# Two attention blocks on one core: another order of TensorE's work in the first block, and a shorter cycle at one place in the second

## The chip, the core and the metric

The kernel runs on one core of a Trainium2 chip. The metric is the device time of one execution in microseconds. Before the change it is 1818.95 us, the median of three runs (1818.33 to 1819.58).

## What is computed

Two independent multi-head attention blocks, A and B, each on an input of 2048 tokens by 512, with 32 heads of 16; their outputs stand beside each other in the result. A looks back over a window of 256 tokens, B looks at all tokens.

```python
qkv = (x @ wqkv).reshape(B, S, 3, H, Dh)             # S=2048, D=512, H=32, Dh=16
scores = einsum("bhqd,bhkd->bhqk", q, k) * Dh**-0.5
# A alone: mask = (i - j >= 0) & (i - j < 256), scores = where(mask, scores, -1e9)
p = softmax(scores, axis=-1)
o = einsum("bhqk,bhkd->bhqd", p, v)                  # then joined over heads
out = o @ wo                                         # result: concat([a, b], -1)
```

## The kernel before

**The work.** The heads are taken in groups of four, the queries in chunks of 512. A unit is (block, group, chunk): 8 groups by 4 chunks make 32 units in A and 32 in B. The work on TensorE comes in four kinds.

- Projections and output products (`products`, L217): matmuls over 128 rows and 512 columns, twelve in a row for one 128x512 tile (four slices, three products each, because every operand is split into a high and a low part). One projection is one letter `p` of the order of block A or, in block B, a tile fed in pieces by the letter `x`.
- Maxima: scores of queries against keys, once over, for the row maximum that softmax subtracts. In A this is `max_item` (L454), read by VectorE (L459, or L463 and L464). In B it is `max2` (L406), read by VectorE's maximum reduction at L410. A large `M` handles two heads at once in two banks of PSUM that are kept for it; a small `m` handles one head in a bank that it shares in turn. The maxima of a unit become rows of its query operand by a small transpose (L492 in A, L539 in B; the letters `t` and `T`).
- Scores (`scores`, L572): the scores again, transposed, with the maxima subtracted by the extra rows. ScalarE takes the exponential of each 128x512 bank (L579); in A GpSimd cuts the edge of the window out of it (L589). These are the letters `s`.
- Weighing (`weigh` L618 in A, `weigh2` L603 in B): the exponentials times the values, four heads in four column groups. These are the letter `w` and, in B, digits that give how many 128-query pieces are weighed.

Scores and maxima use 48 to 51 rows of the array, so two of them run side by side; below, both kinds are called narrow matmuls. Weighing uses 32 columns for each head.

**What sets the order.** The schedule is manual. Every engine gets its instructions in the order in which the Python code issues them, and waits on semaphores alone. Block A follows two written tables: `ORDER_A` (L65) is a string of the letters above, and `ORDER_P` (L50) names the projections, those of B's queries, keys and values among them, in the order in which the `p`s take them. The loop at L964 reads them, and a model of the engines' clocks inside the kernel (class `Model`) decides when loads and the second halves of projections are issued between the letters.

Block B runs in cycles. The loop at L1099 picks one of five strings for each turn: `ORDER`, the plain cycle of two key steps; `ORDER_F`, eight key steps with room for a tile (letters `x`: output products of A); `ORDER_B`, which is the plain cycle without its last `M`; and `LAST` and `LAST_F`, once there are no maxima left. A key step is four scores and four weighing pieces.

```python
ORDER   = "ssm4mssMs2msms2TsM"
ORDER_B = "ssm4mssMs2msms2Ts"
ORDER_F = "msMs2mssm2ssMms4ssMms4 ..."
```

`due()` (L1096) tells whether an output product is to be fed now. A cycle with a tile may only begin when the key step is a multiple of eight. In the kernel before, the key steps go: eleven plain cycles from step 2, sixteen cycles with a tile from step 24, then 170 plain ones, two `LAST` and five `LAST_F`. The rule for `ORDER_B` asked for `due()` at step 22, where it did not hold yet, so that string never stood anywhere.

Of the kernel before, what the change touches and what calls it, by code (L numbers as in the profile page):

```python
# [20 lines left out]
HG = 4  # L21
# [15 lines left out]
STEP = 2.36  # L37
# [3 lines left out]
ORDER = "ssm4mssMs2msms2TsM"  # L41
ORDER_B = "ssm4mssMs2msms2Ts"
ORDER_F = "msMs2mssm2ssMms4ssMms4ssMms4ssMsm4ssMms4mssMsxxxxxxTxxMsmss4MssmsxxxxsMsms4s"
# [4 lines left out]


ORDER_P = (  # L50
# [4 lines left out]
    "Bk31 Bq30 Bq33 Bq32 Bq20 Bk23 Bk30 Bq31 Bk11 Bk33 Bk32 Bq12 ").split()  # L55
FIRST = 4.0
FINAL = 34.5
LOADS = 4.0
# [4 lines left out]


ORDER_A = (  # L65
    "pppppppmpmmpmmpmmmptpmmpmmpsmspmmpmsppmmpmmmpmmtpmsswmmmpsmswtmmpmswssmpmmtpmswmsmpmsswsmwssmpmswmss"
    "wtmmpsmmpsmwmmmpmsmwsmwsstpsmswmmmpsmswwssmpsmsptwsmmpmsmwwmsmpsmsptsmwmsmwsmsmsmwssmmwtssmwmmmpmswm"
    "msptsmmswmmmpmmswsmsmwsmtwsspssmwmmmpmsswtmswmsmpmsswmmswsmmptssmwmmspmsmwmswmsmpsmswmmmptmsmmmpmsmw"
    "smmswmswstmmpmsmsmwsmwsmssmwtmmmpmsmsmwssmwsmtswsmmpmswsmswmmtpsmswmmmpmsswmmmpmmtpsmswwmssptmswsmmw"
    "sspmswmmmpmsswsmtpmmswsmwsmmpmsssmwsmswmmtpssmwmmmpsmswmmmpsmswwsmmptsmwmsmpmsmwmsptsmwmsmpsmsptmswm"  # L70
    "mmpssmwmsmwsmsmwmsmptsmwmsmpsmswmmmpssmwmmmpssmtwwssmpmsswsmwsmmptsewmmmpsempsmswsemwsmptsewmmmpemsp"
    "mmswsmtwssepssmwmmmpempesswemmpssmwwsesptsmwemmpesmwmmpssmwsseptmsmpmmmpesmwsmwsmmpemmpmmmpemmpssmws"
    "mmptsmwmmmpSmSwmSmwSm")
LAND = 700
LATE = 1000
LAND_V = 2000
# [72 lines left out]
def attention_kernel(ctx: ExitStack, tc: tile.TileContext, xT, wqk, wv, wo, out):  # L149
# [9 lines left out]
    M = Model()  # L159
    ready = {}  # L160
    obank = [None]
    ns = 0
# [232 lines left out]
    def max2(g, c, qt, kc, heads, ps):  # L395

        m = maxima(1, g, c).rearrange("p (a r) q k -> p a r q k", a=2)
        early = g == 0 and c == 0 and heads[0] < 2
        if not early:
            follow(("k", 1, g))  # L400
            follow(("q", 1, g, c))
        for n, j in enumerate(heads):
            r, a = divmod(j, 2)
            rows = slice(ROW[a], ROW[a] + KS)
            q, k = (qe[0], ke()) if early else (opq[1, g, c][:, r], opk2(g)[:, r])
            nc.tensor.matmul(ps[:, n], q[rows, 128 * qt:128 * qt + 128], k[rows, kc * QC:kc * QC + QC], start=True,  # L406
                             stop=True)
            t = M.pe("h", 118, 0 if early else loaded(1, g, c))
        r, a = divmod(heads[0], 2)
        nc.vector.tensor_reduce(out=m[:, a:a + len(heads), r, qt, kc], in_=ps, axis=AX.X, op=ALU.max)  # L410
        return M.run("DVE", 65 + 533 * len(heads), t)
# [318 lines left out]
    proj = []  # L730
# [23 lines left out]
    def settle():  # L754

        while soon and soon[0][0] <= M.t["PE"]:
            heapq.heappop(soon)[2]()
# [14 lines left out]
    def room(hold=False):  # L772

        if slot[0]:
            if slot[2] is not None:
                return None, view(("s", slot[2] ^ 1))
            slot[1] ^= 1
            if hold:
                slot[2] = slot[1]
            return None, view(("s", slot[1]))  # L780
        while bank() >= M.NEVER:
            advance()
        b = M.take("e")
        return b, view(b)
# [7 lines left out]
    def pop():  # L792
        now[0], _, f, a = heapq.heappop(todo)
        f(*a)
        made.add((f, *a))

    gen = [None, None]
# [19 lines left out]
    def operands(it):  # L817

        f, b, *a = it
        if f == project_qk:  # L820
            keys = [(("w", b, a[0], a[1]), ("x", b, a[2], i)) for i in range(4)]
            t = slots_st[0] - 2700 + LAND_V
        elif f == project_v:
            keys = [(("w", b, "v", i), ("x", b, a[0], i)) for i in range(4)]
            t = slots_v[0] - 2700 + LAND_V
        else:
            keys = [(("w", b, "o", i), ("o", b, i, a[0])) for i in range(4 if len(a[1]) == 1 else 3)]
            t = 0
        at = [max(ready.get(x, M.NEVER) for x in k) for k in keys]
        return M.NEVER if max(at) >= M.NEVER else max(t, *(x - FEED * i * (f != project_out) for i, x in enumerate(at)))  # L830
# [115 lines left out]
    nm = k = nb = ne = n1 = 0  # L946
# [141 lines left out]
    mx = [(NA + 1 + i // 16, *units[NA + 1 + i // 16][1:], *divmod(i % 16, NQC)) for i in range(16 * turn)]  # L1088
    ns, nq, nm, fed = n1, n1 - 8, AHEADM, 0
    half, odd, full = 2 * AHEADM, None, set()  # L1090
    t0 = M.t["PE"] - 1000 * ns // HG * STEP
    rows, order = [], ORDER
    for u, g, c, qt, kc in mx[:AHEADM]:
        chunk_max(g, c, qt, kc)

    def due():  # L1096
        return gen[0] or proj and proj[0][0] <= ns // HG * STEP and operands(proj[0][3]) <= M.t["PE"]

    while nq < 4 * len(steps):  # L1099
        if nm == len(mx) and len(M.banks["e"]) == 3:  # L1100
            M.banks["e"] += [M.t["PE"] + 4000] * 2
        if nm == len(mx):
            order = LAST_F if due() and not rows else LAST
        else:
            f, g = order == ORDER_F, ns // HG % 8
            order = ORDER_F if due() and g == 0 and nm + 8 <= len(mx) else ORDER
            if order == ORDER and not f and g == 6 and due() and nm + 10 <= len(mx):
                order = ORDER_B
        for x in order:
            k = ns // HG  # L1110
            if x == "s" and k < len(steps):
                if ns % HG == 0:
                    t = k * STEP
                    M.t["PE"] = max(M.t["PE"], t0 + int(1000 * k * STEP))
                    settle()
                    while todo and todo[0][0] <= t:
                        pop()
                scores(1, *steps[k], ns % HG)
                ns += 1
            elif x in "Mm" and (half < 2 * len(mx) or x == "m" and odd is not None):  # L1120
                if x == "M":
                    y = half
                    half += 1
                    max2(*mx[y // 2][1:], (2 * (y % 2), 2 * (y % 2) + 1), ps_all[:, 3:5])
                elif odd is None:
                    y, odd = half, half
                    half += 1
                    max2(*mx[y // 2][1:], (2 * (y % 2),), room()[1][:, None])
                else:
                    y, odd = odd, None  # L1130
                    max2(*mx[y // 2][1:], (2 * (y % 2) + 1,), room()[1][:, None])
                if y != odd:
                    full.add(y)
                while {2 * nm, 2 * nm + 1} <= full:
                    u, g, c, qt, kc = mx[nm]
                    chunk_max(g, c, qt, kc)
                    nm += 1
                    if nm % 16 == 0:
                        low_finish(g, c)
                        rows.append((k + 1, (1, g, c)))  # L1140
            elif x == "T":
                if rows and rows[0][0] + (nm == len(mx)) <= k:
                    max_rows(*rows.pop(0)[1])
            elif x == "x" and (gen[0] or due()):
                now[0] = k * STEP
                advance()
                fed += 1
                if fed == 12:
                    fed = 0
                    advance()  # L1150
                    if nm < len(mx):
                        t0 += 2410
            elif x.isdigit():
                if 0 <= nq < 4 * len(steps):
                    g, c, kt = steps[nq // 4]
                    q = nq % 4
                    weigh2(g, c, kt, 128 * q, 128 * (q + int(x)))
                    if kt == NT - 1 and q + int(x) == 4:
                        unit_end(1, g, c)
                nq += int(x)  # L1160
# [29 lines left out]
```

## Time and profile before

| | |
|---|---|
| runs | 1818.33, 1818.95, 1819.58 us |
| profiled execution, its own time | 1819.65 us |
| its span, first to last instruction | 1817.9 us |
| mean granted TensorE clock | 0.998 |
| TensorE matmul busy | 1798.2 us (99%) |
| VectorE / ScalarE / GpSimd busy | 1515.2 / 1420.0 / 688.8 us |
| block A with the projections | from 10.2 us to about 541 us |
| block B, first plain cycles | about 541 to 592 us |
| block B, cycles with a tile, then plain ones, then the last | from 592 us on |

A busy engine here is one with an instruction under way; matmuls overlap and their ends are modelled, so a stall of TensorE shows in the distance between the starts of its groups better than in the busy time. In the rows of the timeline the first number is the start in us, the second how long the group lasted, and `x8` the number of instructions; a bracket gives the idle time ahead and what ended it.

### The profile page before, as it was taken

How to read it: one execution, taken by the hardware profiler on the slowest of the kernel's cores; microseconds unless marked ns; L12 is line 12 of the kernel's file. 1: busy time of each engine (PE TensorE's matmuls, PEld its weight loads, DVE VectorE, ACT ScalarE, POOL GpSimd, SP SyncE). 2: the span in 40 equal slices, each digit the busy share in tenths (PEclk: the TensorE clock that was granted, in tenths of full speed). 3: DMA queues.
4: the chain of work that ended last, by engine and by line, in shares of the span. 5: the costliest groups of instructions: out<-in, count | busy, mean ns of one | idle time of the engine just before them, and what ended most of it. 6: DMA issues, size and time to landing. Idle time of an engine off the chain costs nothing. (4 is left out here: it accounts for less than half of the span.)

```text
span 1817.9 us, 38163 instructions
## 1 busy us (share of the span) xinstructions
PE 1798.2 (99%) x13992; PEld 901.4 (50%) x13992; DVE 1515.2 (83%) x2189; ACT 1420.0 (78%) x2773; POOL 688.8 (38%) x2054
## 2 busy tenths in 40 slices
PE   7999999999999999999999999999999999999999
PEld 5766666666664444444444444444444444444446
DVE  4655676766689889999989999999999999999911
ACT  4367777565659788888889988998898998899883
POOL 0167787554655453223222423332222333222310
PEclk9999999999999999999999999999999999999999
DMA  7756767454553225111300311030030121000012
GB/s 239 198 177 200 225 206 220 152 164 140 180 182 104 71 74 117 45 42 40 75 28 26 74 47 39 29 78 17 16 76 29 35 63 37 17 24 15 30 34 97
DMA packets 128569, 166.47 MB, mean 92 GB/s; under 512 B 22946, under 2 KB 58258, under 8 KB 128370
## 3 DMA queue, kind: packets, MB, share of 16 engines
q1 hardware_dynamic: 128382, 164.04, 31.2%
q8 instruction: 110, 1.80, 0.4%
q14 instruction: 77, 0.63, 0.1%
HBM read 94.49 MB, written 68.19 MB: 89 GB/s over the span
## 5 line engine op out<-in xcount | busy, mean ns | idle before, releaser
L579 ACT ACTIVATE p<-ps_all 128x512 f32<-128x512 f32 x2432 | 1257.8, 598 | 163.1 <-PE ps_all L572 116.0
L410 DVE TENSOR_REDUCE mt<-ps_all 128x1 f32<-128x512 f32 (+1 forms) x1482 | 1203.4, 884 | 53.3 <-PE ps_all L406 38.2
L572 PE MATMUL ps_all<-oq,opk 51*128 51x512 f32 (+3 forms) x2752 | 739.4, 406 | 2.4 <-ACT p L579 2.1
L406 PE MATMUL ps_all<-opk,oq 48*128 48x512 f32 x2016 | 636.3, 433 | 1.0 <-DVE mt L410 1.0
L603 PE MATMUL ps_all<-p,vt 128*32 128x256 f32 (+1 forms) x5672 | 586.8, 487 | 0.0
L572 PEld LDWEIGHTS ps_all<-oq,opk 51*128 51x128 f32 (+1 forms) x2752 | 376.8, 185 | 227.7 <-ACT p L579 196.0
L406 PEld LDWEIGHTS ps_all<-opk,oq 48*128 48x128 f32 x2016 | 303.1, 185 | 277.7 <-issue 149.7
L517 POOL TENSOR_TENSOR md<-mt,mm 128x4 f32<-128x4 f32 x372 | 75.9, 204 | 612.2 <-DVE mt L410 611.2
L589 POOL TENSOR_SCALAR_AFFINE_SELECT p<-p 128x256 f32<-128x256 f32 x480 | 178.9, 406 | 221.9 <-ACT p L579 220.4
L603 PEld LDWEIGHTS ps_all<-p,vt 128*32 128x32 f32 x5672 | 112.7, 108 | 218.1 <-issue 208.1
L217 PE MATMUL ps_all<-x,w 128*128 128x512 f32 x768 | 195.1, 404 | 10.3 <-ACT w L170 10.2
L463 DVE COPY_PREDICATED ps_all<-mone,ps_all 128x256 f32<-128x256 uint16 x224 | 95.0, 424 | 85.8 <-PE ps_all L454 84.1
L217 PEld LDWEIGHTS ps_all<-x,w 128*128 128x128 f32 x768 | 141.2, 190 | 50.5 <-ACT w L170 10.2
L464 DVE TENSOR_REDUCE mt<-ps_all 128x2 f32<-128x512 f32 x224 | 155.2, 693 | 7.7
L279 ACT ACTIVATE raw<-ps_all 128x512 f32<-128x512 f32 x56 | 33.5, 598 | 108.8 <-PE ps_all L217 105.9
L217 PE MATMUL ps_all<-w_o,x_o 128*128 128x512 f32 x384 | 102.3, 407 | 0.2 <-ACT ob L715 0.2
L217 PE MATMUL ps_all<-w_v,x 128*128 128x512 f32 x384 | 96.4, 400 | 0.3 <-DVE w_v L171 0.3
L618 PE MATMUL ps_all<-p,vt 128*32 128x384 f32 (+2 forms) x1408 | 96.4, 390 | 0.0
L518 POOL TENSOR_SCALAR md<-md 128x4 f32<-128x4 f32 x372 | 81.7, 220 | 32.6
L454 PE MATMUL ps_all<-opk,oq 48*128 48x384 f32 (+2 forms) x512 | 88.1, 373 | 1.3 <-DVE mt L464 1.1
L519 POOL TENSOR_TENSOR mm<-mm,md 128x4 f32<-128x4 f32 x372 | 74.8, 201 | 31.0
L217 PEld LDWEIGHTS ps_all<-w_o,x_o 128*128 128x128 f32 x384 | 68.0, 188 | 26.9 <-issue 8.0
(63 smaller groups left out, 718.3 us busy)
## 6 DMA issues: line engine op xcount, KB each, us to landing
parts<-st SPq DMA_DIRECT2D x64, 512.0 KB
opk<-parts SPq DMA_DIRECT2D x128, 128.0 KB
oq<-parts SPq DMA_DIRECT2D x128, 128.0 KB
od<-ou SPq DMA_DIRECT2D x64, 256.0 KB
vd<-vst SPq DMA_DIRECT2D x32, 272.0 KB
opk<-parts SPq DMA_DIRECT2D x128, 64.0 KB
oq<-parts SPq DMA_DIRECT2D x128, 64.0 KB
t<-od SPq DMA_DIRECT2D x32, 256.0 KB
```

Of the source, the lines that this page charges most:

```text
L217: nc.tensor.matmul(ps, l(u), r(v), start=start and k == 0, stop=stop and k == n - 1)
L406: nc.tensor.matmul(ps[:, n], q[rows, 128 * qt:128 * qt + 128], k[rows, kc * QC:kc * QC + QC], start=True, stop=True)
L410: nc.vector.tensor_reduce(out=m[:, a:a + len(heads), r, qt, kc], in_=ps, axis=AX.X, op=ALU.max)
L454: nc.tensor.matmul(two[:, a, 0:w], opq[b, g, c][rows, r, 128 * qt:128 * qt + 128], opk2(g)[rows, r, t0:t1], start=True, stop=True)
L463: nc.vector.copy_predicated(two[:, :, 256:384], later, two[:, :, 0:128])
L464: nc.vector.tensor_reduce(out=m[:, :, r, qt, 0], in_=two[:, :, 128:384], axis=AX.X, op=ALU.max)
L518: nc.gpsimd.tensor_scalar(d, d, 0.0, None, op0=ALU.max)
L572: nc.tensor.matmul(ps[x][:, col:col + n1], opk2(g)[rows, pr, 128 * k:128 * k + 128], opq[b, g, c][rows, pr, q0:q0 + n1], start=True, stop= ...
L579: nc.scalar.activation(p[:, a0 + x, :w], ps[x][:, :w], AF.Exp, scale=SCALE)
L589: nc.gpsimd.affine_select(out=v, in_=v, pattern=[[0, 2], [sign, 128]], compare_op=ALU.is_ge, fill=zero_fill, base=base, channel_multiplier ...
L603: nc.tensor.matmul(o[32 * j:32 * j + 32, q0:q1], vt[(g // 2) % 2][:, kt, vc:vc + 32], pts[1, g, c, kt, j // 2][:, j % 2, q0:q1], start=kt ...
L618: nc.tensor.matmul(o[32 * j:32 * j + 32, q0:q0 + w], vt[(g // 2) % 2][:, kt, vc:vc + 32], pts[b, g, c, m, j // 2][:, j % 2, col:col + w], ...
```

## The change

Two things change. The tables `ORDER_A` and `ORDER_P` hold another order for block A: the same letters and the same projections, placed differently. And in block B the rule that picks `ORDER_B` looks two key steps ahead and applies once, to the first place that fits.

```diff
 ORDER_P = (
-    "Ak00 Aq00 Av00 Av11 Aq01 Av20 Ak01 Aq02 Av02 Av33 Av13 Ak02 Av03 Av01 Ak03 Av31 Aq03 Av22 Av23 Av21 Av10 "
+    "Ak00 Aq00 Av13 Av03 Aq01 Av12 Aq02 Ak01 Av00 Av22 Av01 Ak02 Av02 Av21 Aq03 Ak03 Av10 Av11 Av32 Av20 Av23 "
...
 ORDER_A = (
-    "pppppppmpmmpmmpmmmptpmmpmmpsmspmmpmsppmmpmmmpmmtpmsswmmmpsmswtmmpmswssmpmmtpmswmsmpmsswsmwssmpmswmss"
+    "pppppppmmpmpmmpmmmptppmmmpsmspmmpmmpmmpmsmtpssmwmsmpsmswwmmmptmswsmmpmsmpmswmmspmsspmmptsmwmmmptsmws"
...
-    rows, order = [], ORDER
+    rows, shorter = [], True
...
-    def due():
-        return gen[0] or proj and proj[0][0] <= ns // HG * STEP and operands(proj[0][3]) <= M.t["PE"]
+    def due(ahead=0):
+        d = (ahead + ahead / 20) * STEP
+        return gen[0] or proj and proj[0][0] <= ns // HG * STEP + d and operands(proj[0][3]) <= M.t["PE"] + 1000 * d
...
-            f, g = order == ORDER_F, ns // HG % 8
+            g = ns // HG % 8
             order = ORDER_F if due() and g == 0 and nm + 8 <= len(mx) else ORDER
-            if order == ORDER and not f and g == 6 and due() and nm + 10 <= len(mx):
-                order = ORDER_B
+            if shorter and g == 6 and due(2):
+                order, shorter = ORDER_B, False
```

In the changed kernel the key steps go: ten plain cycles, one `ORDER_B` at step 22, sixteen cycles with a tile from step 24, 171 plain ones, one `LAST` and five `LAST_F`. The maximum left out at step 22 is made up at the end: every later maximum comes half a letter pair later, and the last ones fall into the plain cycle at step 492.

**TensorE where the first cycle with a tile begins** (step 24 of block B; `oq_0_1` is the query operand of the unit whose scores are made, L572, `oq_0_2` that of the unit whose maxima are made, L406, `p` the exponentials that are weighed, L603). Before:

```order
L603 MATMUL ps_all<-p_0_1_5_0_7005,vt_76 32x256 x2
L603 MATMUL ps_all<-p_0_1_5_1_7018,vt_76 32x256 x2
L572 MATMUL ps_all<-oq_0_1_5847,opk_74 128x512
L406 MATMUL ps_all<-opk_74,oq_0_2_6059 128x512 x3
L572 MATMUL ps_all<-oq_0_1_5847,opk_74 128x512
L406 MATMUL ps_all<-opk_74,oq_0_2_6059 128x512 x2
L572 MATMUL ps_all<-oq_0_1_5847,opk_74 128x512
L603 MATMUL ps_all<-p_0_1_6_0_7034,vt_76 32x256 x2
```

The same place in the changed kernel, between the same two weighing groups:

```order
L603 MATMUL ps_all<-p_0_1_5_0_7005,vt_76 32x256 x2
L603 MATMUL ps_all<-p_0_1_5_1_7018,vt_76 32x256 x2
L572 MATMUL ps_all<-oq_0_1_5834,opk_74 128x512
L406 MATMUL ps_all<-opk_74,oq_0_2_6097 128x512
L572 MATMUL ps_all<-oq_0_1_5834,opk_74 128x512
L406 MATMUL ps_all<-opk_74,oq_0_2_6097 128x512 x2
L572 MATMUL ps_all<-oq_0_1_5834,opk_74 128x512
L603 MATMUL ps_all<-p_0_1_6_0_7034,vt_76 32x256 x2
```

Of the three L406 matmuls after the first score, two are gone: they were the `M` that ended the plain cycle. What stays is the small `m` and the `M` of the cycle with a tile.

**TensorE in block A, scores of group 1, chunk 2** (`oq_1_2`; `oq_2_0` and `oq_2_1` belong to maxima, L454). Before:

```order
L618 MATMUL ps_all<-p_1_2_0_1_1692,vt_76 32x384 x2
L572 MATMUL ps_all<-oq_1_2_1091,opk_75 128x384 x2
L572 MATMUL ps_all<-oq_1_2_1091,opk_75 128x128 x2
L454 MATMUL ps_all<-opk_74,oq_2_0_1455 128x384 x2
L572 MATMUL ps_all<-oq_1_3_1298,opk_75 128x128 x2
L572 MATMUL ps_all<-oq_1_3_1298,opk_75 128x384 x2
L454 MATMUL ps_all<-opk_74,oq_2_0_1455 128x384 x2
L572 MATMUL ps_all<-oq_1_3_1298,opk_75 128x128 x2
L572 MATMUL ps_all<-oq_1_3_1298,opk_75 128x384 x2
L454 MATMUL ps_all<-opk_74,oq_2_1_1622 128x384 x2
L618 MATMUL ps_all<-p_1_2_1_0_1706,vt_76 32x256 x2
```

In the changed kernel, the scores of the same unit:

```order
L454 MATMUL ps_all<-opk_74,oq_2_0_1531 128x384 x4
L572 MATMUL ps_all<-oq_1_2_1115,opk_75 128x256 x4
L217 MATMUL ps_all<-x_0_0_115,w_2_0_953 128x512 x3
L217 MATMUL ps_all<-x_0_1_118,w_2_0_953 128x512 x3
L217 MATMUL ps_all<-x_0_2_123,w_2_0_953 128x512 x3
L217 MATMUL ps_all<-x_0_3_126,w_2_0_953 128x512 x3
L572 MATMUL ps_all<-oq_1_2_1115,opk_75 128x384 x2
L572 MATMUL ps_all<-oq_1_2_1115,opk_75 128x128 x2
L454 MATMUL ps_all<-opk_74,oq_2_0_1531 128x384 x2
L572 MATMUL ps_all<-oq_1_2_1115,opk_75 128x384 x2
L572 MATMUL ps_all<-oq_1_2_1115,opk_75 128x128 x2
L618 MATMUL ps_all<-p_1_2_0_0_1655,vt_76 32x128 x2
```

Before, eighteen narrow matmuls stood in one piece here, with no projection near; now a projection stands between the score steps, and the longest piece of this unit has ten.

More of the change, by code (lines that the diff above doesn't have):

```diff
@@ L50 @@
 ORDER_P = (
[4 rows of a table removed]
-    "Bk31 Bq30 Bq33 Bq32 Bq20 Bk23 Bk30 Bq31 Bk11 Bk33 Bk32 Bq12 ").split()
[4 rows of a table added]
+    "Bq11 Bq20 Bk31 Bq31 Bq13 Bq33 Bk32 Bk33 Bk30 Bk21 Bq32 Bq30 ").split()
 FIRST = 4.0
@@ L65 @@
 ORDER_A = (
-    "pppppppmpmmpmmpmmmptpmmpmmpsmspmmpmsppmmpmmmpmmtpmsswmmmpsmswtmmpmswssmpmmtpmswmsmpmsswsmwssmpmswmss"
[L67 to L73, printed above, removed]
+    "pppppppmmpmpmmpmmmptppmmmpsmspmmpmmpmmmpsmtpssmwmsmpsmswwmmmptmswsmmpmsmpmswmmspmsspmmptsmwmmmptsmws"
+    "mmpsmswsmwmsmptmswmsmwsspsmswmmmpsmswmswmmmptwssmpmsspmmswmmpsmswtmswmmspsmswmmsptsmwmsmwsmsmwssmwmm"
+    "spmmtpsmswmmmptmsswmmswswssspmmswmmwmspssmwmsmpmsswtmmmpmmspsmmwswmmmptsmsmwmsmptsmswmmmpsmmswmmswst"
+    "smswsmswmspmsmmwmswtssmwsmmpsmsmwmmswsmmswmmmptssmwmsmptsmsmwsmswmmmpmsswsmmpmswmmsptmswsmmpmmswmmpm"
+    "sswmswmsmptsmwmmmpssmpmmtpmmswsmwsmmpsmswsmswmmtpsmswmmmpsmswtsmswmswmsspsmwmsswsmwmsmptsmswmmmpsmsw"
+    "ssmwtmmmpsmmpmswmmmpmsstwsmswmmmpmsswmmmpmmtpsmmptmswmswsempmswsmmpmmswwesmpessptmswsmmpmsmwmswsemps"
+    "sewemsptssmwemmpseswmmmpesswsmswwsempmmtpemspseswsmwmmmpsempmmmpemmptssmwmmmpseswsewmmmpmmmpsmstwmsm"
+    "psmswmmmpmmSwSwmmSpSm")
 LAND = 700
```

6 rows, old and new, of the table ORDER_P are left out of this document.

## The prediction

> **What bounds the kernel now.** I read the page first, then the windows by stage, then TensorE's timeline wherever the distance between two starts was longer than elsewhere.
>
> ```profile
> span 1817.9 us, 38163 instructions
> PE 1798.2 (99%) x13992; PEld 901.4 (50%) x13992; DVE 1515.2 (83%) x2189; ACT 1420.0 (78%) x2773; POOL 688.8 (38%) x2054
> ```
>
> TensorE is the bound: 99% of the span. The same matmuls run before and after the change, so time can only come from stalls of TensorE, from its clock, and from the small price of going from one kind of matmul to another. The windows say where the stalls are.
>
> ```profile
> 100.00:160.00 60.00, 60.00 (x496) 39.70 (x495) 33.91 (x71) 39.59 (x78) 39.67 (x79) 1.00 0.63 193
> 160.00:280.00 120.00, 117.86 (x987) 75.59 (x988) 86.44 (x207) 88.19 (x175) 93.72 (x177) 1.00 0.68 206
> 280.00:540.00 260.00, 259.78 (x1998) 172.27 (x1996) 179.89 (x337) 156.87 (x309) 147.47 (x295) 1.00 0.56 172
> 592.00:604.00 12.00, 11.00 (x64) 4.09 (x62) 8.90 (x11) 6.48 (x13) 8.19 (x16) 0.72 0.26 67
> 1100.00:1300.00 200.00, 200.00 (x1721) 84.19 (x1714) 200.00 (x261) 180.20 (x355) 61.60 (x246) 1.00 0.14 37
> ```
>
> The columns are the window, its length, then busy time of PE, PEld, DVE, ACT and POOL, and near the end the granted clock. Two places stand out: 160 to 280 us in block A, and the twelve microseconds from 592, where the mean clock was 0.72. The plain cycles (1100 to 1300) have no idle TensorE, and a VectorE that is busy throughout: there the two are level.
>
> **The seam at 592 us.** Here the plain cycles end and the first cycle with a tile begins. TensorE's timeline:
>
> ```profile
> 590.22 0.64 PE L603 MATMUL ps_all<-p,vt 128*32 128x256 f32 x8
> 590.79 0.50 PE L406 MATMUL ps_all<-opk,oq 48*128 48x512 f32 x1
> 591.46 0.64 PE L603 MATMUL ps_all<-p,vt 128*32 128x256 f32 x8
> 592.03 0.50 PE L572 MATMUL ps_all<-oq,opk 51*128 51x512 f32 x1
> 592.03 0.94 PE L406 MATMUL ps_all<-opk,oq 48*128 48x512 f32 x3
> 592.81 0.40 PE L572 MATMUL ps_all<-oq,opk 51*128 51x512 f32 x1
> 594.21 0.50 PE L406 MATMUL ps_all<-opk,oq 48*128 48x512 f32 x2 [1.00 <-DVE mt L410]
> 594.55 0.40 PE L572 MATMUL ps_all<-oq,opk 51*128 51x512 f32 x1
> 594.88 0.64 PE L603 MATMUL ps_all<-p,vt 128*32 128x256 f32 x8
> 598.82 1.93 PE L603 MATMUL ps_all<-p,vt 128*32 128x512 f32 x8
> 600.69 0.79 PE L572 MATMUL ps_all<-oq,opk 51*128 51x512 f32 x2
> 603.46 0.50 PE L572 MATMUL ps_all<-oq,opk 51*128 51x512 f32 x2
> 604.36 1.07 PE L603 MATMUL ps_all<-p,vt 128*32 128x512 f32 x8
> 605.36 0.50 PE L572 MATMUL ps_all<-oq,opk 51*128 51x512 f32 x2
> ```
>
> At 594.21 the large `M` of the new cycle waits for VectorE: the plain cycle's last `M` (the L406 at 592.03) still holds the two banks. VectorE had no gap since 584.76, and a large reduction takes 1.22 us:
>
> ```profile
> 584.76 12.51 DVE L410 TENSOR_REDUCE mt<-ps_all 128x1 f32<-128x512 f32 x16
> 598.51 1.82 DVE L410 TENSOR_REDUCE mt<-ps_all 128x2 f32<-128x1024 f32 x2 [1.24 <-PE ps_all L406]
> ...
> L410 DVE TENSOR_REDUCE mt<-ps_all 128x2 f32<-128x1024 f32 x566 | 687.6, 1217 | 51.7 <-PE ps_all L406 38.0 <-PE ps_all L572 7.9
> ```
>
> What came after is odd: the same weighing of eight 512-column matmuls took 1.87 us (598.82 to 600.69) and 1.00 us later (604.36 to 605.36). Windows cut at the change of clock:
>
> ```profile
> 592.49:595.90 3.41, 2.41 (x20) 1.04 (x17) 3.41 (x4) 1.79 (x3) 3.19 (x4) 1.00 0.56 143
> 595.90:599.31 3.41, 3.41 (x22) 1.22 (x22) 2.16 (x4) 2.32 (x5) 3.09 (x7) 0.50 0.20 70
> 599.31:602.73 3.42, 3.42 (x18) 1.03 (x14) 1.80 (x3) 1.56 (x4) 1.51 (x5) 0.50 0.00 0
> 602.73:606.14 3.41, 3.41 (x28) 1.18 (x20) 2.87 (x5) 2.19 (x5) 0.00 (x0) 1.00 0.00 0
> ```
>
> The granted clock fell to 0.50 for 6.83 us, right after 3.41 us in which TensorE was busy for 2.41 (71%). So the stall costs twice: itself, and the slow clock behind it. It is the only slow stretch once the work runs: 6.83 us at half clock make 0.998 of the span's mean, which is what the run lists:
>
> ```profile
> core 0: 1817.9 us, clock 0.998
> ```
>
> **The change, term by term.**
>
> *The stall at the seam, -1.7 us.* Prices of undisturbed visits: narrow matmuls, four of them, 0.67 us (590.79 to 591.46); six of them, 0.90 (603.46 to 604.36). That is 0.20 for a visit and 0.235 for each pair side by side. The eight from 592.03 should have taken 0.20 + 4 x 0.235 = 1.14 and took 2.85 (to 594.88): 1.71 too long. With `ORDER_B` ahead, the `M` that held the banks is gone. The `M` before that is older, VectorE has 1.22 us less ahead of it, and the wait falls away; what is late next is the same VectorE, by at most what is left of its queue: 0 to 0.5 us, and I take 0. The pair of matmuls (0.235 us) is not saved, only made up at the end.
>
> *The slow clock, -3.0 us.* From 594.88 to 604.36 stand two 256-column weighings, two of 512 columns, four narrow matmuls once and six three times. At full clock: 2 x 0.57 (590.22 to 590.79) + 2 x 1.00 + 0.67 + 3 x 0.90 = 6.51 us. They took 9.48: 2.97 lost. If the clock stays up, all of it comes back, as VectorE even idled there (1.24 us at 598.51). From above the term is bounded by half of 6.83, 3.4 us; from below by nothing, if the clock falls all the same. I take 3.0, since the drop sits exactly behind the one window with so much idle TensorE.
> [...]
>
> *Block A's stalls, -1.5 us.* They come where many narrow matmuls stand in one piece, because ScalarE and VectorE cannot empty the banks as fast. In the order there are eight pieces of 12 to 18, all between 170 and 392 us. The first and the last:
>
> ```profile
> 168.95 0.44 PE L454 MATMUL ps_all<-opk,oq 48*128 48x384 f32 x2
> 169.83 1.07 PE L618 MATMUL ps_all<-p,vt 128*32 128x128 f32 x16
> 170.83 0.50 PE L572 MATMUL ps_all<-oq,opk 50*128 50x384 f32 x4
> 173.48 1.07 PE L618 MATMUL ps_all<-p,vt 128*32 128x256 f32 x16
> ...
> 389.71 0.50 PE L572 MATMUL ps_all<-oq,opk 50*128 50x256 f32 x4
> 391.35 1.07 PE L618 MATMUL ps_all<-p,vt 128*32 128x128 f32 x16
> ```
>
> Eight matmuls took 0.88 us (168.95 to 169.83) without a stall; the eighteen from 170.83 took 2.65, some 0.7 to 1.1 too long; the twelve from 389.71 took 1.64, about 0.5 too long. Worked out so for all eight pieces, about 6.4 us are lost. The new order has six such pieces, all of twelve. At the mean of the three old twelves (0.57) they lose 3.4: a gain of 2.9. Against it: the stretches without any projection that are longer than the usual are as many as before (seven over 5 us of work, where there were six, though the longest has 44 narrow matmuls and not 60), and by their length the loss would hardly change. Half of 2.9 is my value; the ends are -4 and +1.5.
>
> *More visits, +1.3 us.* In the order of the whole program there are five more visits to weighing and three more to narrow matmuls. A visit to weighing costs 2 x 0.57 - 1.00 = 0.14 us beyond its columns, one to narrow matmuls 0.20: 5 x 0.14 + 3 x 0.20 = 1.3. This is queued on TensorE itself, and nothing hides it.
>
> *The end of the maxima, 0.* There the exponentials bind for some steps:
>
> ```profile
> 1732.47 0.99 PE L572 MATMUL ps_all<-oq,opk 51*128 51x512 f32 x2 [0.21 <-ACT p L579]
> 1735.57 0.50 PE L572 MATMUL ps_all<-oq,opk 51*128 51x512 f32 x1 [0.45 <-ACT p L579]
> ```
>
> Before, two `LAST` steps in a row push four scores each through three banks; after, one `LAST` follows a plain cycle that is nearly empty of maxima, three steps instead of two, but in smaller pieces. Between -0.9 and +0.9; I take 0. The last tail of 134 output products is the same in both orders.
>
> Sum: -1.7 - 3.0 - 1.5 + 1.3 + 0 = -4.9 us. Against the profiled execution's own 1819.65 us (span 1817.9 and 1.75 around it) that is 1814.75. This execution lies 0.7 above the median of the runs, 1818.95; from the median it is 1814.05, and I say 1814.1.
>
> **The rivals.** A measurement of this kernel can tell about 0.2%, 3.6 us: faster means under 1815.3, slower over 1822.6.
>
> 1. *The clock falls anyway.* The slow stretch has another cause than the stall, or some other stall of the seam is enough for it. For it: 1.0 us of idle is little. Against: no other stretch has a slow clock, and no other wait of TensorE shown here is as long; where it idled 0.21 and 0.45 us at 1732.47 and 1735.57, the clock stayed. Then -1.9: 1817.0, no change.
> 2. *Block A's new order pays nothing.* For it speak the visits and the stretches without projections, against it the shorter pieces. Then block A's stalls change by 0 to +1.5 and the sum is -3.4 to -1.9: 1815.6 to 1817.0, no change.
> 3. *Slower: block A falls into the slow clock itself.* Its place is 160 to 280 us, where ScalarE, VectorE and GpSimd are busiest and TensorE waits most. If the new order crowds the stalls, a window of 3.41 us with 71% of busy TensorE halves the clock for two windows: a stall of 1.0 and 3.0 behind it. One such dip makes 1818, no change; it decides the sign from three on: 1814.1 + 3 x 4 = 1826. Against it: the new order's pieces are shorter, and the old one, with eighteen in a piece, never fell so far.
>
> That the shorter cycle does not stand where it should is excluded by the order shown above.
>
> **How the numbers follow.** My forecast, all terms about as taken, 0.60; rival 1, 0.12; rival 2, 0.24; rival 3, 0.04. The time is that of the forecast, 1814.1. The range goes down to the forecast with block A's stalls at -4 and some of the end's gain, 1810.8, and up past rivals 1 and 2 with a microsecond for what a run differs, 1818.0. Faster by over 0.2%: 0.60, the forecast. No change: rivals 1 and 2, 0.36. Slower: 0.04.
>
> **What would show it.** Right: at the first cycle with a tile the narrow matmuls run without a bracket for VectorE, in about 0.9 us for six; the granted clock is 1.00 from the start of work to the end, and the mean over the seam's twelve microseconds with it; block B is shorter by about 4.5 us from its first weighing on, block A by nearly nothing. Wrong: a window at 0.50 anywhere behind the start; new waits in block A of over a microsecond each; or a block B that is shorter by 1.7 us only.

## The result, and the profile after

The changed kernel takes 1835.28 us (median of four runs, 1834.08 to 1835.92) against 1819.05 for the kernel before beside it (four runs, 1818.33 to 1819.58): ratio 1.0089, 95% interval 1.0071 to 1.0106. It is 16 us slower; 5 us faster was forecast, and the range ended at 1818.0.

The page of the profiled execution (its own time 1834.83 us), and the windows by stage with the same columns as before:

```profile
span 1833.1 us, 38164 instructions
PE 1794.1 (98%) x14000; PEld 897.7 (49%) x14000; DVE 1515.7 (83%) x2190; ACT 1424.6 (78%) x2773; POOL 692.3 (38%) x2054
```

```profile
160.00:280.00 120.00, 119.06 (x1020) 77.33 (x1020) 83.15 (x193) 89.70 (x178) 96.12 (x178) 1.00 0.72 214
280.00:540.00 260.00, 259.48 (x1997) 171.35 (x1989) 183.07 (x341) 157.99 (x313) 149.76 (x305) 1.00 0.58 174
590.00:602.00 12.00, 12.00 (x97) 4.53 (x95) 11.71 (x15) 10.32 (x20) 8.17 (x16) 1.00 0.21 60
1100.00:1300.00 200.00, 195.64 (x1682) 81.34 (x1674) 195.60 (x256) 177.02 (x346) 61.05 (x243) 1.00 0.13 35
```

The two places that the prediction spoke of got better. Block A has less idle TensorE between 160 and 280 us (0.9 us where it was 2.1). At the seam TensorE is busy for all twelve microseconds, at a clock of 1.00 (0.72 before). What got worse is the row of the plain cycles, whose letters were not changed: TensorE and VectorE each stand still there for 4.4 of 200 us, and before the change neither did.

The seam on TensorE's timeline of the changed kernel: the six narrow matmuls from 592.26 to 593.16 take 0.90 us and have no bracket, which is what the prediction asked for.

```profile
591.69 0.64 PE L603 MATMUL ps_all<-p,vt 128*32 128x256 f32 x8
592.26 0.51 PE L572 MATMUL ps_all<-oq,opk 51*128 51x512 f32 x2
592.60 0.63 PE L406 MATMUL ps_all<-opk,oq 48*128 48x512 f32 x3
592.84 0.40 PE L572 MATMUL ps_all<-oq,opk 51*128 51x512 f32 x1
593.16 1.06 PE L603 MATMUL ps_all<-p,vt 128*32 128x512 f32 x8
```

Who makes TensorE stand still is in the list of waits (total us, times, longest). Before, the transposition L539 (the letter `T`) waited once for GpSimd:

```profile
PE ps_all L539 <- POOL nm L529: 0.5, 1, 0.5
```

After, 29 of the 31 transpositions wait:

```profile
PE ps_all L539 <- POOL nm L529: 20.0, 29, 2.2
```

**One unit, before and after.** Once all maxima of a unit are reduced, GpSimd works through a chain (L517, L518, L519, then L526 to L529) that ends in `nm`, and `T` turns `nm` into rows of the query operand. Before, from the timeline:

```profile
1135.27 0.20 POOL L517 TENSOR_TENSOR md<-mt,mm 128x4 f32<-128x4 f32 x1 [1.53 <-DVE mt L410]
1136.97 0.22 POOL L529 TENSOR_TENSOR nm<-nr,nm 128x16 bf16<-128x16 f32 x1
1137.66 0.24 PE L539 MATMUL ps_all<-ident,nm 128*48 128x128 bf16 x1
```

After:

```profile
1137.34 0.21 POOL L517 TENSOR_TENSOR md<-mt,mm 128x4 f32<-128x4 f32 x1 [1.53 <-DVE mt L410]
1139.04 0.22 POOL L529 TENSOR_TENSOR nm<-nr,nm 128x16 bf16<-128x16 f32 x1
1139.32 0.24 PE L539 MATMUL ps_all<-ident,nm 128*48 128x128 bf16 x1 [0.74 <-POOL nm L529]
1140.25 4.15 DVE L410 TENSOR_REDUCE mt<-ps_all 128x2 f32<-128x1024 f32 x5 [0.73 <-PE ps_all L572]
```

The chain is as long as it was: 1135.27 to 1137.19 (1.92 us) and 1137.34 to 1139.26 (1.92). Before, `T` stood 0.47 us behind its end. After, TensorE reached `T` at 1138.58 (1139.32 less the 0.74 of the bracket), 0.68 us ahead of the end of the chain. Measured from the chain's start, the place of `T` moved from 2.39 us behind it to 1.24: the maxima of the unit are complete 1.15 us later, in the same order of letters. The reason is a parity. A plain cycle makes four halves of a letter pair, `mm`, `M`, `mm`, `M`, and a unit has 32 halves, so that a unit always ended on the last `M` of one cycle, and its `T` stood in the next. With one `M` left out at the seam, every unit ends on the first `mm` of the cycle in which its own `T` stands. The last row shows what follows: `T` holds up the narrow matmuls behind it on TensorE, the maxima among them, so that the bank that VectorE reads next is filled later (the bracket names L572, the scores that run beside those maxima; L410 reads the banks that L406 writes). VectorE had no idle time in the plain cycles before (busy for 200.00 of 200 us between 1100 and 1300), and loses 0.73 us here.

**The account by stage**, from the starts of the first weighing of block B, of the second and of the next to last transposition. Before:

```profile
540.87 1.06 PE L603 MATMUL ps_all<-p,vt 128*32 128x512 f32 x8
...
611.62 0.24 PE L539 MATMUL ps_all<-ident,nm 128*48 128x128 bf16 x1
...
1698.46 0.24 PE L539 MATMUL ps_all<-ident,nm 128*48 128x128 bf16 x1
```

After:

```profile
538.24 1.07 PE L603 MATMUL ps_all<-p,vt 128*32 128x512 f32 x8
...
604.57 0.24 PE L539 MATMUL ps_all<-ident,nm 128*48 128x128 bf16 x1 [0.30 <-POOL nm L529]
...
1711.59 0.24 PE L539 MATMUL ps_all<-ident,nm 128*48 128x128 bf16 x1 [0.72 <-POOL nm L529]
```

| stage | before, us | after, us | difference |
|---|---|---|---|
| block A, up to the first weighing of B | 540.87 | 538.24 | -2.6 |
| from there over the seam to the second transposition | 70.75 | 66.33 | -4.4 |
| to the next to last transposition | 1086.84 | 1107.02 | +20.2 |
| to the end of the span | 119.44 | 121.51 | +2.1 |
| sum, as the spans | 1817.9 | 1833.1 | +15.2 |

### The profile page after: what moved, and what is told of

Same layout as the page of the kernel before. It is cut to its first block, busy times and chain, and to the rows that moved or that the text cites. A ratio compares the mean times of both kernels' runs of the same rounds, so it can differ in the third digit from the quotient of the medians.

```text
span 1833.1 us, 38164 instructions
## 1 busy us (share of the span) xinstructions
PE 1794.1 (98%) x14000; PEld 897.7 (49%) x14000; DVE 1515.7 (83%) x2190; ACT 1424.6 (78%) x2773; POOL 692.3 (38%) x2054
## 5 line engine op out<-in xcount | busy, mean ns | idle before, releaser
L410 DVE TENSOR_REDUCE mt<-ps_all 128x1 f32<-128x512 f32 (+1 forms) x1483 | 1203.9, 887 | 75.7 <-PE ps_all L406 47.9
L572 PE MATMUL ps_all<-oq,opk 51*128 51x512 f32 (+3 forms) x2752 | 740.4, 404 | 0.6 <-ACT p L579 0.2
L406 PE MATMUL ps_all<-opk,oq 48*128 48x512 f32 x2016 | 631.3, 432 | 0.3 <-ACT p L579 0.3
L603 PE MATMUL ps_all<-p,vt 128*32 128x256 f32 (+1 forms) x5680 | 585.9, 485 | 1.4 <-ACT ou L629 1.4
L572 PEld LDWEIGHTS ps_all<-oq,opk 51*128 51x128 f32 (+1 forms) x2752 | 377.4, 185 | 221.4 <-ACT p L579 185.6
L406 PEld LDWEIGHTS ps_all<-opk,oq 48*128 48x128 f32 x2016 | 299.4, 184 | 277.3 <-DVE mt L410 161.5
L517 POOL TENSOR_TENSOR md<-mt,mm 128x4 f32<-128x4 f32 x372 | 76.5, 206 | 579.2 <-DVE mt L410 577.1
L603 PEld LDWEIGHTS ps_all<-p,vt 128*32 128x32 f32 x5680 | 112.5, 108 | 219.8 <-issue 207.9
L518 POOL TENSOR_SCALAR md<-md 128x4 f32<-128x4 f32 x372 | 82.3, 221 | 32.7
L514 POOL TENSOR_SCALAR mm<-mt 128x4 f32<-128x4 f32 x124 | 28.8, 232 | 171.9 <-DVE mt L410 171.8
L519 POOL TENSOR_TENSOR mm<-mm,md 128x4 f32<-128x4 f32 x372 | 75.5, 203 | 31.0
L454 PE MATMUL ps_all<-opk,oq 48*128 48x384 f32 (+2 forms) x512 | 85.6, 372 | 1.2 <-DVE mt L464 0.8
```

Source lines behind the costliest of these rows:

```text
L454: nc.tensor.matmul(two[:, a, 0:w], opq[b, g, c][rows, r, 128 * qt:128 * qt + 128], opk2(g)[rows, r, t0:t1], start=True, stop=True)
L518: nc.gpsimd.tensor_scalar(d, d, 0.0, None, op0=ALU.max)
L572: nc.tensor.matmul(ps[x][:, col:col + n1], opk2(g)[rows, pr, 128 * k:128 * k + 128], opq[b, g, c][rows, pr, q0:q0 + n1], start=True, stop= ...
L603: nc.tensor.matmul(o[32 * j:32 * j + 32, q0:q1], vt[(g // 2) % 2][:, kt, vc:vc + 32], pts[1, g, c, kt, j // 2][:, j % 2, q0:q1], start=kt ...
```

## The experiments

The theory, W: `T` waits for GpSimd because each unit's last maximum comes one half later. Its rivals were O, that the new order of block A does the damage, and V, that the missing `M` leaves VectorE and TensorE out of step whatever `T` does. Beside the first four experiments the kernel before took 1820.04 us (17 runs), beside the last three 1819.77 (16 runs).

**Order alone.** The new tables without the shorter cycle:

```diff
-    rows, shorter = [], True
+    rows, shorter = [], False
```

> The new order of block A alone; the shorter cycle never stands. Theory W (the small transposition of block B waits for GpSimd, because the shorter cycle lets each unit's last maximum come one large reduction later): no such waits, so the stall and the slow clock at the seam are back and only block A's gain is left, 1819.05 - 2.6 = 1816.4 us, range 1815 to 1818. Rival O (the new order of block A upsets block B): the loss stays, 1832 us or more.

Measured: 1816.98 us (ten runs, 1813.31 to 1817.97), ratio 0.9984, interval 0.9975 to 0.9994. One transposition waits, for 0.5 us, as before. Rival O falls: the new order gains 3 us.

**Shorter cycle alone.** The new rule for `ORDER_B`, with both tables as they were before:

```diff
 ORDER_P = (
-    "Ak00 Aq00 Av13 Av03 Aq01 Av12 Aq02 Ak01 Av00 Av22 Av01 Ak02 Av02 Av21 Aq03 Ak03 Av10 Av11 Av32 Av20 Av23 "
+    "Ak00 Aq00 Av00 Av11 Aq01 Av20 Ak01 Aq02 Av02 Av33 Av13 Ak02 Av03 Av01 Ak03 Av31 Aq03 Av22 Av23 Av21 Av10 "
...
```

> The old order of block A, with the shorter cycle at step 22. Theory W: all of the loss is here, 1835.3 + 2.6 = 1837.9 us, range 1836 to 1840, the transposition waits about 0.73 us in each unit of the plain cycles, and no slow clock at the seam. Rival O: the shorter cycle saves its 4.7 us, 1814 us.

Measured: 1838.94 us (four runs), ratio 1.0107, interval 1.0092 to 1.0122. The waits are those of the whole change:

```profile
PE ps_all L539 <- POOL nm L529: 18.6, 29, 1.2
```

**Transposition later.** The changed kernel with `T` in the plain cycle behind the first `m` of the cycle that follows, so that GpSimd's chain is done when TensorE gets there:

```diff
-ORDER = "ssm4mssMs2msms2TsM"
+ORDER = "ssmT4mssMs2msms2sM"
```

> The changed kernel with the letter T of the plain cycle moved behind the next cycle's first three letters, about 0.9 us later; nothing else. Theory W: the wait of about 0.73 us in some 21 units of the plain cycles goes, VectorE has no gap of 0.73 us per unit any more, and the time falls by about 15 us to 1820 us, range 1817 to 1822 (the waits in the cycles with a tile stay). Rival V (VectorE and TensorE fall out of step because the queue of VectorE was shortened, and the transposition's wait is only a sign of it): still 1833 us or more, the gaps of VectorE move to another place.

Measured: 1824.14 us (eight runs), ratio 1.0025, interval 1.0014 to 1.0035. That is above the expected 1817 to 1822. Of the 16 us, 12 are back. `T`'s waits now:

```profile
PE ps_all L539 <- POOL nm L529: 4.6, 8, 2.2
PE ps_all L539 <- ACT p L579: 4.6, 22, 0.2
```

In the plain cycles no transposition waits for GpSimd any more; each meets another wait, 0.2 us for an exponential of ScalarE, at its new place, which the expectation had not counted. The cycles with a tile hold a `T` of their own in `ORDER_F`, which was not moved; there the waits stay. V is hard to keep: the same `M` is missing here, and most of the loss is gone.

**Transposition earlier.** The kernel before, with neither new tables nor a shorter cycle, and `T` two small maxima earlier:

```diff
-ORDER = "ssm4mssMs2msms2TsM"
+ORDER = "ssm4mssMs2Tmsms2sM"
```

> The kernel before with the letter T of the plain cycle moved 1.2 us ahead; no shorter cycle, old order. The slack of the transposition behind GpSimd there is 0.47 us, so theory W expects a wait of about 0.75 us in some 20 units: 1819.05 + 15 = 1834 us, range 1831 to 1837. Rival V: the queue of VectorE is not shortened, 1819 us.

Measured: 1836.55 us (four runs), ratio 1.0099, interval 1.0082 to 1.0116. Nothing of the change is in this kernel, and its plain units have the same wait, at the same place:

```profile
1137.37 0.22 POOL L529 TENSOR_TENSOR nm<-nr,nm 128x16 bf16<-128x16 f32 x1
1137.63 0.24 PE L539 MATMUL ps_all<-ident,nm 128*48 128x128 bf16 x1 [0.74 <-POOL nm L529]
...
1138.33 1.29 DVE L410 TENSOR_REDUCE mt<-ps_all 128x1 f32<-128x512 f32 x2 [0.48 <-PE ps_all L572]
```

Here `T` was brought forward against the maxima, there the maxima were pushed back against `T`. That alone is enough for 16.5 us. That the whole change loses nearly as much is partly luck: it loses more, also in the cycles with a tile and at the end, and has gains to set against it.

**The left-out maximum made up.** The changed kernel with one more `M` in the first cycle with a tile, between the products, which puts the parity back:

```diff
-            order = ORDER_F if due() and g == 0 and nm + 8 <= len(mx) else ORDER
+            order = (ORDER_F.replace("MsxxxxxxTxxM", "MsxxxMxxxTxxM") if half % 2 else ORDER_F) if due() and g == 0 and nm + 8 <= len(mx) else ORDER
```

> The changed kernel with one thing more: the reduction that the shorter cycle leaves out is made up in the first cycle with a tile (a third M there, between the tile's products), so that the later maxima again come where they came in the kernel before. If the transposition waits for GpSimd only because a unit's last maximum comes one half of a letter pair later, the waits for GpSimd go from the third unit on (at most 1 us of them left in all), VectorE has no gaps of 0.7 us between 945 and 1700 us, and the gains remain: the kernel before, about 1819 to 1820 on its chip, less 2.9 for the new order of block A (1820.04 to 1816.98) and less 4.7 for the stall and the slow clock at the seam, plus up to 0.8 for the made-up reduction's visit between the products: 1813, range 1811 to 1815. If the waits come from the orders of the first block or from the missing visit at the seam, about 1830 to 1835 as the changed kernel.

Measured: 1814.28 us (five runs, 1812.28 to 1814.59), ratio 0.9966, interval 0.9954 to 0.9979: faster than either kernel, by 5.5 us against before. The transposition waits once, as before, and a large maximum once:

```profile
PE ps_all L406 <- DVE mt L410: 0.6, 1, 0.6
PE ps_all L539 <- POOL nm L529: 0.5, 1, 0.5
```

Its stages, from the rows

```profile
538.27 1.06 PE L603 MATMUL ps_all<-p,vt 128*32 128x512 f32 x8
...
604.34 0.49 PE L406 MATMUL ps_all<-opk,oq 48*128 48x512 f32 x2 [0.65 <-DVE mt L410]
...
605.66 0.24 PE L539 MATMUL ps_all<-ident,nm 128*48 128x128 bf16 x1
...
1692.48 0.24 PE L539 MATMUL ps_all<-ident,nm 128*48 128x128 bf16 x1
```

are 538.27, 67.39, 1086.82 and (to its span of 1812.1) 119.62 us: against before -2.6, -3.4, 0.0 and +0.2. The long stage is that of before to a few hundredths. The made-up `M` costs about a microsecond of the seam's gain, 0.65 of it in the row at 604.34: a large maximum again waits for VectorE, now between the products.

**Made up earlier.** The same with the added `M` in another part of that cycle:

```diff
-            order = (ORDER_F.replace("MsxxxxxxTxxM", "MsxxxMxxxTxxM") if half % 2 else ORDER_F) if due() and g == 0 and nm + 8 <= len(mx) else ORDER
+            order = (ORDER_F.replace("ssmsxxxxsMs", "ssmsxxMxxsMs") if half % 2 else ORDER_F) if due() and g == 0 and nm + 8 <= len(mx) else ORDER
```

> As the run with the made-up reduction between the products, but with it placed earlier in the first cycle with a tile, in that cycle's first half. If only the parity of the maxima matters, the waits go as there, and the time is within 1.5 us of that run (1812 to 1815); if the place itself matters (VectorE still busy with the maxima of the seam, TensorE waiting for its next banks), a few us more. If the parity isn't the cause, 1830 to 1835.

Measured: 1814.47 us (six runs, 1813.43 to 1814.73), ratio 0.9969, interval 0.9957 to 0.9981. Between these two places the place does not matter; the parity does.

**Made up, with the old tables.** The line of the first made-up kernel, with `ORDER_A` and `ORDER_P` as before the change.

> The old order of block A and of the projections, with the shorter cycle and the made-up reduction: the seam's part of the change alone, without the late maxima. If the late maxima are the whole loss of the shorter cycle (1838.94 against 1820.04 without the make-up), 1820 less 4.7 for the stall and the slow clock at the seam, plus up to 0.8 for the visit: 1816, range 1814 to 1818. If something else in the shorter cycle costs, above 1822.

Measured: 1816.41 us (eleven runs, 1815.31 to 1817.75), ratio 0.9983, interval 0.9974 to 0.9991. The seam's part alone gains 3.4 us. With the 3.1 of the order alone that makes 6.4, and both together measured 5.5; the intervals, about 2 us on either side, do not tell these apart.

The starts of the second, the ninth and the next to last transposition in the traces show where each kernel loses, in us:

| stage | before | changed | `T` later | `T` earlier | made up |
|---|---|---|---|---|---|
| second to ninth transposition, cycles with a tile | 297.5 | 301.9 | 301.8 | 297.5 | 297.5 |
| ninth to next to last, nearly all plain cycles | 789.3 | 805.2 | 794.0 | 804.8 | 789.3 |

Rival V is refuted by the two kernels with a moved `T`. With `T` later the `M` is missing as in the changed kernel, and of the 15.9 us lost in the plain cycles 11.2 are back; the 4.7 that are left are about the 21 waits of 0.2 us for ScalarE. With `T` earlier no `M` is missing, and 15.5 us are lost there. The kernels that make the `M` up do not tell V from W, because they take away the cause that either names; they show that the loss goes with the left-out half.

How VectorE loses what TensorE waits, in one row each: its maximum reductions between 945 and 1700 us, with busy time, mean, and the idle time ahead of them. First before, then the changed kernel, the transposition moved later, and the maximum made up:

```profile
L410 DVE TENSOR_REDUCE mt<-ps_all 128x1 f32<-128x512 f32 (+1 forms) x970 | 754.4, 857 | 0.1
```

```profile
L410 DVE TENSOR_REDUCE mt<-ps_all 128x2 f32<-128x1024 f32 x951 | 739.9, 861 | 14.7 <-PE ps_all L572 13.2 <-PE ps_all L406 1.5
```

```profile
L410 DVE TENSOR_REDUCE mt<-ps_all 128x1 f32<-128x512 f32 (+1 forms) x966 | 752.0, 861 | 2.6 <-PE ps_all L572 0.2
```

```profile
L410 DVE TENSOR_REDUCE mt<-ps_all 128x1 f32<-128x512 f32 (+1 forms) x970 | 754.0, 859 | 0.1
```

## Why the prediction was wrong

- **The step that failed** is in the term of the stall: the pair of matmuls "is not saved, only made up at the end". It priced the 0.235 us that a pair of maxima takes on TensorE, and put at nothing that the results of all later maxima come later. It named nobody who waits for a unit's last maximum, though GpSimd's chain and `T` do. The numbers were in the trace of before: `T` stood 0.47 us behind a chain of 1.92, and two small reductions, which now come ahead of a unit's end, take 1.2 to 1.3 us on VectorE (the row of two at 1138.33 above, 1.29). An estimate from these, 1.2 to 1.3 less 0.47, is 0.7 to 0.8 us in each plain unit. Measured were a shift of 1.15 us and 21 waits of 0.68 to 0.74; with seven of 0.30 to 0.46 and one of 2.2 in the cycles with a tile they are the 20 us of the list of waits. What made the one of 2.2 so long was not followed up.
- **That VectorE and TensorE are level in the plain cycles** was read rightly and not used. Neither had idle time there to make up a delay with: 21 waits of about 0.73 us are 15.3, and the stage of the plain cycles got 15.9 us longer.
- **The stall at the seam, -1.7, and the slow clock, -3.0:** right at the seam. The six narrow matmuls take their 0.90 us, the clock stays at 1.00 in the profiled execution, and the stage is 4.4 us shorter although a wait of 0.30 stands at its end. Rival 1 did not come there. Two of the changed kernel's four executions list a mean clock of 0.999 all the same, which the forecast of a clock of 1.00 to the end did not allow for; the last section comes back to it. The gain holds only as long as the left-out maximum stays unpaid: made up in time, it leaves 3.4.
- **Block A, -1.5 and some of the +1.3 for visits:** the two together were forecast at -0.2, and block A ended 2.6 us earlier. That is more than the forecast, which took half of 2.9 for the stalls, and inside its ends. The order alone gained 3.1 (interval 1 to 5). Rival 2, that it pays nothing, is out; rival 3, a slow clock in block A, did not come (1.00 from 160 to 540 us).
- **The end of the maxima, 0 between -0.9 and +0.9:** also wrong. The last stage is 2.1 us longer, and 0.2 with the maximum made up. In it TensorE is busy for 116.0 us where it was busy for 115.0, with 60 matmuls of maxima for 58, and idle for 1.0 us more. The list of waits of the changed kernel has a line there that the list of before has not, a weighing that stands for ScalarE (at 1761.30 us): `PE ps_all L603 <- ACT ou L629: 1.4, 1, 1.4`. Against these 1.4 us the waits for exponentials in that stage fall from 0.7 to 0.2. The same line stands in the lists of the shorter cycle alone and of the transposition moved later, and in none of the kernels that leave no maximum unpaid. Why ScalarE is late there was not tried.
- **The rivals** held a slower case of 1826 us with 4%, by another mechanism in another block. The one that came was not among them: what is late after a later maximum was asked only at the seam itself, where the answer was the same VectorE, and not for the thirty units behind it. Rival 3 reckoned with the clock halved behind any 3.41 us with 71% of busy TensorE. The trace of before shows that at the seam; in the order alone the same 1.00 us of idle TensorE stood at a clock that stayed at 1.00 (last section).

The sum of the forecast, 1814.1, is by coincidence close to that of the kernel with the maximum made up (1814.28): a larger gain in block A and a smaller one at the seam.

## What to carry to other kernels

Leaving out or moving one step of a sequence that runs on with a counter moves all later results (here by 1.15 us). For each consumer at a fixed place, read its slack in the trace (here 0.47 us between the end of GpSimd's chain and `T`) and compare it with the shift before anything else is priced; what is missing, times the number of times it comes round, was here nearly the whole cost, with TensorE and VectorE both without idle time before: 21 times about 0.73 us are 15.3, of 15.9. If the step can be made up before the next consumer, the shift stays local: here one reduction put back within 13 us turned 16 us of loss into 5.5 of gain.

## What the runs showed of the clock

The slow clock behind the seam's stall is not fixed to it. Of the 33 executions of the kernel before that ran beside the experiments, 32 have a mean clock of 0.998 or 0.999 and take 1818.29 to 1821.11 us; one has 1.000 and takes 1816.77. Of the ten of the order alone, nine have 0.998 (1816.48 to 1817.97 us) and one 1.000 (1813.31). This last one was profiled, and it has the same stall of one microsecond:

```profile
591.12 0.50 PE L406 MATMUL ps_all<-opk,oq 48*128 48x512 f32 x2 [1.00 <-DVE mt L410]
```

```profile
588.00:600.00 12.00, 11.00 (x88) 4.46 (x85) 11.64 (x14) 9.15 (x18) 8.62 (x18) 1.00 0.34 84
```

The clock stayed at 1.00. So the price of the slow stretch is about 3 to 4 us by one execution of each kernel (1820.04 to 1816.77, 1816.98 to 1813.31), near the 3.0 that was worked out from durations. With the stall in the order, the mean clock is below 1.000 in 41 of these 43 executions and 1.000 in two. All 22 executions of the three kernels with the maximum made up, whose longest wait at the seam is 0.65 us, have 1.000.

Slow stretches came without a stall of one microsecond too. Where the `M` is left out and not made up, the seam has no such stall, and yet the mean clock is below 1.000 in two of four executions of the changed kernel, in two of four of the shorter cycle alone, and in all eight of the transposition moved later. The traces of the latter two kernels show it near the end, where the maxima run out: 0.50 for 3.41 us, from 1753.9 us in the one and from 1738.9 in the other, each right behind 3.41 us in which TensorE was busy for 3.20 and 3.21 (94%) and idle for 0.2. The changed kernel's own trace shows no such stretch. So 3.41 us with 1.0 and with 0.2 us of idle TensorE stood right ahead of a slow stretch in these traces, and the 1.0 us in the trace of the order alone had none behind it. Whether the idle time is what lowers the clock, and what decides when it does, no run here shows.
